# A two-layer network and a long convolution on one core: when the filter's first matrices are requested, in which order a block's rows are scaled, which engine writes zero rows, and where the plan pauses

## The chip, the core and the metric

The kernel runs on one core of one Trainium2 chip. The core has TensorE (matrix multiplication, with a weight load ahead of each product), VectorE, ScalarE, GpSimd, and SyncE, which here only issues DMAs. The profile calls them PE (weight loads PEld), DVE, ACT, POOL and SP. Each engine takes its instructions in an order that is fixed when the program is built, and waits for semaphores of the others.

The metric is the device time of one execution in microseconds, lower is better.

## The reference

With x of 2048 rows and 576 columns, all in float32:

```python
x = A_q
xn = _layernorm(x, axis=-1)
return x + _A_ref(xn, A_k, A_v, A_shift_k, A_ssm_k, A_ssm_D) + _B_ref(xn, B_w1, B_w2)
```

`_B_ref` is `relu(xn @ w1) @ w2` with w1 of 576 x 4608 and w2 of 4608 x 576. `_A_ref` is a gated long convolution: k goes through a causal convolution of four taps per column, the result is multiplied by v, then convolved per column over all 2048 rows with the filter `ssm_k` (the reference does so by an FFT of 4096 points), `ssm_D` times its input is added, and q, here the normalized x, multiplies the result.

## The kernel before, in words

**Number format.** Each float32 operand of TensorE is split into a high and a low part, and a product is made of three matmuls (high x high, high x low, low x high). ScalarE writes the high part, VectorE or, for weights, GpSimd the low part (`split_lo`, line 417).

**The layers.** Rows stand in four blocks of four tiles of 128 rows (`BT`). A visit (the loop of line 1130) takes one block through 256 of the 4608 columns of w1: `mm1` (line 538) for blocks 0 and 1, or `quad` (line 566), which saves products by sums of quarters, for blocks 2 and 3. `relu` (line 526) splits the result. `unit` (line 593) then multiplies 128 rows with a half of w2 (288 columns) and adds the sum onto `acc`; `done["acc"]` is the latest of these sums, `done["act"]` the latest ScalarE step of a visit.

**The first two blocks.** `first_xT` (line 231) centres and turns block 0 at the start. `second_xT` (line 279) does so for block 1 during the second visit: four rows are scaled by `normalized` (line 186) over all 576 columns, one after the other; then `turned` (line 267) transposes one column block of 128 of all four rows on TensorE into a bank, and `split_low` (line 210) writes its high part on ScalarE (line 219) and its low part on VectorE (line 220). Later blocks go through `later_xT` (line 292), in steps spread over many visits.

**The convolution** is a generator, `conv` (line 670), with four stages that run between the matmuls of the layers:
- the filter's transform (lines 709 to 766): `ssm_k` is loaded in twelve pieces, three matrices are requested by `load_const` (line 645) from GpSimd's queue, and after a pause 64 steps of `first` (line 656) follow, each of two matmuls, with a further matrix requested after each pair;
- the rows' transform (lines 769 to 847): `tap` makes the short convolution on VectorE (lines 788, 791, 792), `gate` multiplies by v (line 797), `split` writes the operands (lines 807 to 814), and `first` transforms them. The first loads for it (`first_loads`, line 702, and `load`, line 691) are emitted shortly before the end of the stage ahead. For the three rows before the start, `load` writes a zero into the first partition (line 698) and loads the rest;
- the middle (lines 850 to 951): 34 passes with products (line 879) over the transforms of filter and rows;
- the way back (lines 954 to 1033): `load_z` and `load_rest` fetch operands, lines 1020 and 1021 multiply them, `gate` and `add` finish.

**The plan.** `tick` (line 1045) is called after each six or seven matmuls of the layers with their columns as cost. It advances the clock and, where the convolution has credit, takes at most one step of the generator. A step that yields a positive number spends that many units of credit; one that yields a negative number stops the generator until so many columns of layer work have gone by. A unit of credit accrues at `rate` (line 1038):

```python
rate = FFT_TOTAL / (SHARE * FFN_TOTAL - PAUSES * PAUSE - START)
```

So the W_ constants (line 55) set how the convolution's steps are spread, and the pauses where it holds still. `PAUSE` is 16000 columns.

**Order.** The program's order of emission is a priority: the builder lets each engine take the earliest emitted instruction that it holds ready, and this fixes the engine's order. `tc.issue_after(x)` puts the instructions in its block behind x on x's engine; `here()` (line 664) puts them behind the latest sum on VectorE and the latest ScalarE step. A one-column memset in front of a DMA, as on line 715, ties that DMA to such a place, since the DMA then has to wait for it.

Of the kernel before, what the change touches and what calls it, by code (L numbers as in the profile page):

```python
# [17 lines left out]
P = 128  # L18
S = 2048
D = 576  # L20
# [3 lines left out]
NH = D // 2  # L24
# [7 lines left out]
BT = T // NB  # L32
# [5 lines left out]
U = S // (T * A1)  # L38
# [10 lines left out]
PAUSE = 16000  # L49
# [2 lines left out]


N_FK, N_FX, N_FM, N_FO = 4 * T, 4 * T, 6 * NG, 4 * T
W_FK, W_FX, W_FM, W_FO = 1.25, 4.7, 1.55, 2.35
Q = 32
KB = 3
KT_GAP = 2000
PAUSES = 4 * NH // Q // KB * KT_GAP / PAUSE + 13
FFT_TOTAL = N_FK * W_FK + N_FX * W_FX + N_FM * W_FM + N_FO * W_FO  # L60
W_QUAD = sum(W_STAGE)
FFN_TOTAL = NPAIR * HB * (W_PLAIN + W_QUAD + 2 * 4 * W_UNIT)
# [47 lines left out]
def h3_ffn_kernel(ctx: ExitStack, tc, x, k, v, shift_k, ssm_k, ssm_D, w1, w2, fwd, inv, mid, out):  # L110
    nc = tc.nc
# [16 lines left out]
    mv = const.tile([P, T, 2], F32, name="mv")  # L128
    rstd = const.tile([P, T], F32, name="rstd")
# [39 lines left out]
    def stats(t, src):  # L169
        st = xp.tile([P, 2, 6], F32, tag="bn", name=f"bn{t}", bufs=4)  # L170
        for h in range(2):
            nc.vector.bn_stats(st[:, h, :], src[:, h * NH:(h + 1) * NH])
        nc.vector.bn_aggr(mv[:, t, :], st)

    def inv_std(t0, n):

        q = xp.tile([P, 3, BT], F32, tag="q", name=f"q{t0}")[:, :, :n]
        va, h0, qu = q[:, 0, :], q[:, 1, :], q[:, 2, :]
        nc.vector.tensor_scalar(va, mv[:, t0:t0 + n, 1], EPS, None, op0=OP.add)
        nc.scalar.activation(h0, va, AF.Sqrt, scale=0.25)  # L180
        nc.vector.reciprocal(qu, h0)
        nc.vector.tensor_tensor(qu, va, qu, OP.mult)
        nc.vector.scalar_tensor_tensor(qu, qu, 0.25, h0, op0=OP.mult, op1=OP.add)
        nc.vector.reciprocal(rstd[:, t0:t0 + n], qu)

    def normalized(dst, src, t):
        nc.vector.tensor_scalar(dst, src, mv[:, t, 0:1], rstd[:, t:t + 1],
                                op0=OP.subtract, op1=OP.mult)

    def centred(dst, src, t):  # L190
# [7 lines left out]
    def f32(t):  # L198
        return t.bitcast(F32)
# [23 lines left out]
    def row_tiles(s, name):  # L223
        t = scratch(s, name)
        return [t[:, i * D:(i + 1) * D] for i in range(BT)]

    def plain_tiles(s):
        for name in ("b1", "b2", "xr"):
            operand(s, name)
# [37 lines left out]
    def turned(c, xn):  # L267
        w = min(P, D - c * P)
        ps = fft_psum()
        for i in range(BT):  # L270
            nc.tensor.transpose(ps[:w, i * P:(i + 1) * P], xn[i][:, c * P:c * P + w], ident)
        return ps
# [6 lines left out]
    def second_xT(srcs):  # L279

        plain_tiles(1)
        with tc.issue_after(done["acc"].ins):
            for t in range(BT + 2, HT):
                stats(t, srcs[t])
            inv_std(BT, BT)
        xn = row_tiles(1, "xn1")
        for i, row in enumerate(xn):
            normalized(row, srcs[BT + i], BT + i)
        for c in range(5):
            split_low(c, turned(c, xn), 1)  # L290

# [350 lines left out]
            unit(*args)  # L642
            room -= size

    def load_const(pool, src, name):
        w = pool.tile([P, 2, P], F32R, tag="wt", name=name, bufs=3)
        nc.gpsimd.dma_start(w, src)
        return w

# [13 lines left out]
    @contextmanager  # L663
    def here():


        with tc.issue_after(done["acc"].ins), tc.issue_after(done["act"].ins):
            yield

    def conv():  # L670
# [5 lines left out]
        with hold_pool as kp:  # L676
# [3 lines left out]
            win, gates, sums, uses = {}, {}, {}, [0]  # L680

            def slot(i):
                return both[:, i * D:(i + 1) * D]
# [7 lines left out]
            def load(t):  # L691
                win[t] = slot(WIN + t % (KS + 1))
                if t >= 0:
                    move(win[t], k, t, queues=(nc.sync, nc.sync))
                    gates[t] = slot(GATE + t % 2)
                    move(gates[t], v, t, queues=(nc.sync, nc.sync))
                else:
                    nc.vector.memset(win[t][0:1, :], 0.0)
                    nc.sync.dma_start(win[t][1:A1, :], k[1, 0:A1 - 1, T + t, :])
                    nc.sync.dma_start(win[t][A1:, :], k[0, :, T + t, :])  # L700

# [7 lines left out]
            with tc.tile_pool(name="fk", bufs=2) as fp:  # L709
                skip = fp.tile([P, NH], F32, tag="z", name="skip", bufs=3)  # L710
                for h in range(2):
                    nc.sync.dma_start(skip[h * A1:h * A1 + 1, :], ssm_D[None, h * NH:(h + 1) * NH])
                for b in range(0, NH // Q, KB):
                    with here():
                        nc.vector.memset(kr[:, b:b + KB, :1], 0.0)  # L715
                    for q in range(4):
                        h, r = divmod(q, 2)
                        src = ssm_k[h * NH + b * Q:h * NH + (b + KB) * Q, r * 32 * A2:(r + 1) * 32 * A2]
                        nc.sync.dma_start(kr[q * Q:(q + 1) * Q, b:b + KB, :],
                                          src.rearrange("(b d) l -> d b l", d=Q))  # L720
                        yield -KT_GAP
                ws = {}
                for n in range(3):
                    ws[n] = load_const(fp, fwd[n // U][:, n % U], f"wk{n}")
                yield -PAUSE
                turned_ = {}

                def transpose(i):
                    t2 = order[i]
                    pool, tag = (xp, "m5") if i % 2 else (fp, "tr")  # L730
                    tr = turned_[i] = pool.tile([P, NH], F32, tag=tag, name=f"tr{t2}", bufs=1)
                    with here():
                        nc.vector.transpose(tr.rearrange("p (b q) -> p b q", q=Q),
                                            kr.rearrange("p b (q t) -> p b q t", t=A2)[:, :, :, t2])
                        if t2 == 0:
                            for h in range(2):
                                row = slice(h * A1, h * A1 + 1)
                                nc.vector.tensor_tensor(tr[row, :], tr[row, :], skip[row, :], OP.add)

                def prepare(i, h):  # L740
                    if h == 0:
                        transpose(i)
                    stk = fp.tile([P, NH], F32R, tag="stk", name=f"ks{order[i]}_{h}", bufs=3)
                    with here():
                        stack(stk, turned_[i], h)
                    return stk

                order = [T * u + t for t in range(T) for u in range(U)]
                nxt = []
                for h in range(2):  # L750
                    nxt.append(prepare(0, h))
                    yield -PAUSE / 8
                for n, t2 in enumerate(order):
                    stk, nxt = nxt, []
                    u, t = divmod(t2, T)
                    for h in range(2):
                        z = fp.tile([P, NH], F32, tag="z", name=f"zk{t2}_{h}", bufs=3)
                        first(ws[n], stk[h], z, u)
                        nc.sync.dma_start(zk[:, t2, h * NH:(h + 1) * NH], z)
                        if n + 1 < len(order):  # L760
                            nxt.append(prepare(n + 1, h))
                        yield W_FK
                    if n + 2 == len(order):
                        first_loads()
                    if n + 3 < len(order):
                        ws[n + 3] = load_const(fp, fwd[(n + 3) // U][:, (n + 3) % U], f"wk{n + 3}")


            with tc.tile_pool(name="fx", bufs=2) as fp:
# [43 lines left out]
                            own, other = halves(u)  # L813
                            nc.sync.dma_start(f32(stks[t, u])[other], sums[t][own])

                yield -4 * PAUSE
                for n in range(KS):
                    tap(0, n)
                    yield -PAUSE / 4
# [7 lines left out]
                for t in range(T):  # L827
# [7 lines left out]
                    for u in range(U):  # L835
                        for h in range(2):
                            cols = slice(h * NH, (h + 1) * NH)
# [7 lines left out]
                        n = U * t + u + 3  # L845
# [4 lines left out]
        with tc.tile_pool(name="fm", bufs=2) as fp:  # L850
# [44 lines left out]
            for g in range(NG + 2):  # L895
# [10 lines left out]
                for h in range(2):  # L906
                    if g < NG:
                        ps, cols = run(*parts["k", g], 0, h)
# [6 lines left out]
                if 0 <= xg < NG:  # L915
                    k1, k2 = ks_.pop(xg)
                    sw = fp.tile([P, D], F32, tag="sw", name=f"sw{xg}", bufs=1)
                    for h in range(2):
                        ps, cols = run(*parts["x", xg], 0, h)
# [10 lines left out]
                for h in range(2):  # L930
                    if back is not None:
                        ps, cols = run(*back, 1, h)
# [21 lines left out]
        with tc.tile_pool(name="fo", bufs=2) as fp:  # L954
# [48 lines left out]
                load_z(n)  # L1003
            for i in range(2):
                load_rest(i)
            yield -3 * PAUSE / 2
            for n, (t, u) in enumerate(units):
                i = n // U
                w = rest[i][0]
# [5 lines left out]
                for h in range(2):  # L1015
# [3 lines left out]
                    cols = slice(h * NH, (h + 1) * NH)  # L1019
# [14 lines left out]


    stream = conv()
    clock = {"ffn": 0.0, "conv": 0.0, "until": START, "done": False}
    rate = FFT_TOTAL / (SHARE * FFN_TOTAL - PAUSES * PAUSE - START)

# [90 lines left out]
    for q, (n, s) in enumerate(visits):  # L1130
# [3 lines left out]
        if q == 1:  # L1134
            fill()
            second_xT(acc)
# [65 lines left out]
```

## Time and profile before

| | us |
|---|---|
| median of 3 runs | 1076.67 |
| lowest and highest | 1075.96, 1077.86 |
| the profiled execution | 1073.58 |
| its span, first to last instruction | 1071.8 |
| VectorE, ScalarE, GpSimd busy in the span | 753.2, 548.4, 394.1 |

The span leaves out what lies before the first and after the last instruction of the program, so it is shorter than the time of the same execution. The profile is of one execution, and the median is of others, so a term found in the profile is a difference that is applied to the median. In the page's rows a line such as L610 is line 610 of the kernel, `a<-b` names the tile written and the tile read, and a bracket in a timeline gives the idle time of the engine ahead of that instruction and what ended it. Matmuls overlap in the profile: one of 288 columns shows some 0.29 us, while a run of 24 takes 3.19 us.

### The profile page before, as it was taken

How to read it: one execution, taken by the hardware profiler on the slowest of the kernel's cores; microseconds unless marked ns; L12 is line 12 of the kernel's file. 1: busy time of each engine (PE TensorE's matmuls, PEld its weight loads, DVE VectorE, ACT ScalarE, POOL GpSimd, SP SyncE). 2: the span in 40 equal slices, each digit the busy share in tenths (PEclk: the TensorE clock that was granted, in tenths of full speed). 3: DMA queues.
4: the chain of work that ended last, by engine and by line, in shares of the span. 5: the costliest groups of instructions: out<-in, count | busy, mean ns of one | idle time of the engine just before them, and what ended most of it. 6: DMA issues, size and time to landing. Idle time of an engine off the chain costs nothing.

```text
span 1071.8 us, 19954 instructions
## 1 busy us (share of the span) xinstructions
PE 1051.1 (98%) x7147; PEld 988.1 (92%) x7147; DVE 753.2 (70%) x1310; ACT 548.4 (51%) x1201; POOL 394.1 (37%) x395
## 2 busy tenths in 40 slices
PE   8999999999999999999999999999999999999998
PEld 5799999889899999999999999999999999999997
DVE  5437878889777787762487777787878774566764
ACT  4224566535333344332386777777787763443430
POOL 4122333233222223233434434443434343544541
PEclk9999999999999999999999999999999999999999
DMA  8564867787847656855985556655655647977834
GB/s 215 125 160 127 223 159 197 199 260 205 211 139 207 185 170 193 247 154 184 315 233 180 159 156 180 191 170 168 191 162 162 182 122 242 315 246 221 239 124 111
DMA packets 156303, 204.45 MB, mean 191 GB/s; under 512 B 32845, under 2 KB 122703, under 8 KB 155180
## 3 DMA queue, kind: packets, MB, share of 16 engines
q1 hardware_dynamic: 143308, 189.00, 59.6%
q0 software_dynamic: 12576, 13.44, 5.4%
q8 instruction: 56, 0.92, 0.4%
q10 hardware_dynamic: 320, 0.74, 0.3%
q14 instruction: 43, 0.35, 0.1%
HBM read 133.92 MB, written 55.05 MB: 176 GB/s over the span
## 4 chain that ended last, share of the span: by engine, by line
PE 86%; DMA 7%; DVE 2%; ACT 1%; issue 1%; SPq 1%; POOL 0%; POOLq 0%; DVEq 0%; ACTq 0%
PE pso L610 38%; PE psh L547 20%; PE psb L523 12%; PE psf L879 6%; PE psa L523 5%; PE psf L660 3%; DMA zo<-zy 1%; DMA r<-in_w 1%; DMA both<-in_k 1%; DMA b<-kept_b 1%; DMA xt<-in_x 1%; PE psf L1020 1%; DMA ztk<-zk 1%; PE psf L1021 1%; DMA fin<-acc 1%
## 5 line engine op out<-in xcount | busy, mean ns | idle before, releaser
L610 PE MATMUL pso<-w,hh 128*128 128x288 f32 x2304 | 469.1, 295 | 2.1 <-DVE acc L614 1.6
L610 PEld LDWEIGHTS pso<-w,hh 128*128 128x128 f32 x2304 | 372.8, 188 | 11.4 <-DVE acc L614 2.3
L610 PE MATMUL pso<-w,ll 128*128 128x288 f32 x1152 | 328.1, 295 | 0.5 <-DVE both L715 0.5
L418 POOL TENSOR_TENSOR g<-r,g 128x256 fp32r<-128x256 f32 (+2 forms) x145 | 168.8, 1169 | 402.1 <-ACT g L447 326.5
L547 PE MATMUL psh<-b,g 128*128 128x512 f32 x864 | 217.8, 395 | 0.9 <-ACT b L219 0.7
L610 PEld LDWEIGHTS pso<-w,ll 128*128 128x128 f32 x1152 | 212.7, 188 | 1.5 <-DVE both L715 0.7
L547 PEld LDWEIGHTS psh<-b,g 128*128 128x128 f32 x864 | 157.1, 188 | 31.5 <-ACT b L219 1.2
L618 DVE TENSOR_TENSOR acc<-pso,acc 128x288 f32<-128x288 f32 x224 | 98.6, 450 | 69.3 <-PE pso L610 68.1
L418 POOL TENSOR_TENSOR w<-r,w 128x576 fp32r<-128x576 f32 x72 | 113.6, 1578 | 54.6 <-ACT w L509 54.4
L529 ACT ACTIVATE hh<-psh 128x512 fp32r<-128x512 f32 x72 | 43.0, 598 | 145.2 <-PE psh L547 145.0
L530 DVE SCALAR_TENSOR_TENSOR ll<-psh,hh 128x512 fp32r<-128x512 f32 x72 | 49.5, 688 | 69.3 <-ACT hh L529 69.1
L523 PE MATMUL psb<-t,g 128*128 128x256 f32 x648 | 95.0, 281 | 0.3 <-DVE psa L578 0.3
L447 ACT ACTIVATE g<-r 128x256 fp32r<-128x256 f32 (+2 forms) x145 | 76.7, 542 | 26.2 <-DMA r<-in_w 18.5
L523 PEld LDWEIGHTS psb<-t,g 128*128 128x128 f32 x648 | 85.4, 188 | 0.8 <-DVE psa L578 0.7
L476 POOL TENSOR_TENSOR r<-r 128x256 f32<-128x256 f32 x72 | 59.4, 845 | 44.5 <-DMA r<-in_w 43.3
L523 PE MATMUL psa<-b,g 128*128 128x256 f32 x432 | 63.4, 281 | 0.3 <-ACT psa L574 0.3
L523 PE MATMUL psb<-b,g 128*128 128x256 f32 x432 | 58.6, 281 | 0.0
L523 PEld LDWEIGHTS psa<-b,g 128*128 128x128 f32 x432 | 56.8, 188 | 0.6 <-ACT psa L574 0.6
L523 PEld LDWEIGHTS psb<-b,g 128*128 128x128 f32 x432 | 54.9, 188 | 0.0
L922 DVE TENSOR_TENSOR k<-psf,k 128x288 f32<-128x288 f32 x64 | 29.0, 454 | 33.8 <-ACT sw L921 32.1
L614 DVE SCALAR_TENSOR_TENSOR acc<-pso,rstd,acc 128x288 f32<-128x288 f32 x80 | 40.6, 511 | 16.8 <-PE pso L610 16.3
L529 ACT ACTIVATE hh<-psa 128x512 fp32r<-128x512 f32 x36 | 21.5, 596 | 53.8 <-PE psa L523 53.5
(133 smaller groups left out, 1684.2 us busy)
## 6 DMA issues: line engine op xcount, KB each, us to landing
r<-in_w SPq DMA_DIRECT2D x72, 288.0 KB, 3.6
zy<-vo SPq DMA_DIRECT2D x64, 288.0 KB, 3.2
zo<-zy SPq DMA_DIRECT2D x32, 576.0 KB, 5.6
r<-in_w SPq DMA_DIRECT2D x35, 512.0 KB, 4.0
zk<-zk SPq DMA_DIRECT2D x64, 144.0 KB, 2.6
ztk<-zk SPq DMA_DIRECT2D x32, 288.0 KB, 3.0
ztx<-zx SPq DMA_DIRECT2D x32, 288.0 KB, 3.2
k<-k SPq DMA_DIRECT2D x64, 144.0 KB, 3.0
```

The costliest lines, as they stand in the source:

```text
L418: return nc.gpsimd.tensor_tensor(dst, src, hi, OP.subtract)
L447: nc.scalar.activation(hi, src, AF.Copy)
L476: nc.gpsimd.tensor_tensor(dst, a, b, op)
L523: nc.tensor.matmul(ps, a, m, start=start and i == 0, stop=i == len(seq) - 1, skip_group_check=not start)
L529: done["act"] = nc.scalar.activation(hh, ps, AF.Relu)
L530: lows.append(nc.vector.scalar_tensor_tensor(ll, ps, 0.0, hh, op0=OP.max, op1=OP.subtract))
L547: nc.tensor.matmul(ps, a, m, start=i == 0, stop=i == len(seq) - 1)
L610: nc.tensor.matmul(ps[:, :NH], a, m, start=c == 0, stop=c == len(seq) - 1)
L614: done["acc"] = nc.vector.scalar_tensor_tensor(acc[t][:, dc], ps[:, :NH], rstd[:, t:t + 1], acc[t][:, dc], op0=OP.mult, op1=OP.add)
L618: done["acc"] = nc.vector.tensor_tensor(acc[t][:, dc], ps[:, :NH], acc[t][:, dc], OP.add)
L660: nc.tensor.matmul(ps[:, :NH], w[:, n, :], stk, start=n == 0, stop=n == 1)
L879: nc.tensor.matmul(ps[:, :NH], a, m[:, cols], start=n == 0, stop=n == 2)
```

## The change

Five things are altered. `load_const` gets a switch `late`, with which a one-column memset on VectorE, placed behind the latest sum, comes ahead of the request; the filter's first three matrices use it. `second_xT` scales the leading 128 columns of all four rows first, and then the other 448 of each. The memset of the zero rows goes from VectorE to GpSimd. Two pauses are longer by half a `PAUSE` each, ahead of the short convolution and ahead of the way back, and `PAUSES`, the constant that the rate takes off for them, is larger by one. The weights of a step of the filter's transform and of the rows' transform go from 1.25 to 1.3 and from 4.7 to 4.65.

```diff
-W_FK, W_FX, W_FM, W_FO = 1.25, 4.7, 1.55, 2.35
+W_FK, W_FX, W_FM, W_FO = 1.3, 4.65, 1.55, 2.35
...
-PAUSES = 4 * NH // Q // KB * KT_GAP / PAUSE + 13
+PAUSES = 4 * NH // Q // KB * KT_GAP / PAUSE + 14
...
-    def normalized(dst, src, t):
-        nc.vector.tensor_scalar(dst, src, mv[:, t, 0:1], rstd[:, t:t + 1],
+    def normalized(dst, src, t, cols=slice(0, D)):
+        nc.vector.tensor_scalar(dst[:, cols], src[:, cols], mv[:, t, 0:1], rstd[:, t:t + 1],
                                 op0=OP.subtract, op1=OP.mult)
...
         xn = row_tiles(1, "xn1")
-        for i, row in enumerate(xn):
-            normalized(row, srcs[BT + i], BT + i)
+        for cols in (slice(0, P), slice(P, D)):
+            for i, row in enumerate(xn):
+                normalized(row, srcs[BT + i], BT + i, cols)
...
-    def load_const(pool, src, name):
+    def load_const(pool, src, name, late=False):
         w = pool.tile([P, 2, P], F32R, tag="wt", name=name, bufs=3)
+        if late:
+            with here():
+                nc.vector.memset(f32(w)[:, 0, :1], 0.0)
         nc.gpsimd.dma_start(w, src)
         return w
...
-                    nc.vector.memset(win[t][0:1, :], 0.0)
+                    nc.gpsimd.memset(win[t][0:1, :], 0.0)
...
-                    ws[n] = load_const(fp, fwd[n // U][:, n % U], f"wk{n}")
+                    ws[n] = load_const(fp, fwd[n // U][:, n % U], f"wk{n}", late=True)
...
-                yield -4 * PAUSE
+                yield -9 * PAUSE / 2
...
-            yield -3 * PAUSE / 2
+            yield -2 * PAUSE
```

## The prediction

> **What bounds the kernel now.** First the head of the page: engines, clock, and the chain that ended last.
>
> ```profile
> span 1071.8 us, 19954 instructions
> PE 1051.1 (98%) x7147; PEld 988.1 (92%) x7147; DVE 753.2 (70%) x1310; ACT 548.4 (51%) x1201; POOL 394.1 (37%) x395
> PEclk9999999999999999999999999999999999999999
> PE 86%; DMA 7%; DVE 2%; ACT 1%; issue 1%; SPq 1%; POOL 0%; POOLq 0%; DVEq 0%; ACTq 0%
> ```
>
> TensorE is busy in 1051.1 of 1071.8 us at its full granted clock, and 86% of the chain is matmuls. The change removes no matmul, so all it can win lies in the 20.7 us in which TensorE stood, and some of those are the fill at the front and the last stores. Where they stand is read from the windows (columns: the stretch, its length, then TensorE, its weight loads, VectorE, ScalarE and GpSimd busy, clock, DMA share and GB/s) and from TensorE's own list of waits (total, times, longest).
>
> ```profile
> 0.00:13.50 13.50, 9.69 (x47) 5.06 (x47) 3.41 (x10) 6.04 (x12) 5.97 (x14) 1.00 0.93 225
> 13.50:34.00 20.50, 16.75 (x89) 13.18 (x90) 17.70 (x50) 6.67 (x15) 5.87 (x5) 1.00 0.86 209
> 205.00:275.00 70.00, 67.03 (x399) 60.21 (x398) 61.64 (x97) 29.41 (x60) 22.71 (x22) 1.00 0.83 243
> 520.00:890.00 370.00, 367.76 (x2797) 361.62 (x2796) 280.53 (x484) 263.41 (x589) 151.11 (x129) 1.00 0.59 176
> 890.00:1055.00 165.00, 162.51 (x1240) 159.50 (x1239) 101.98 (x190) 65.13 (x150) 80.10 (x91) 1.00 0.74 227
> ```
>
> ```profile
> PE psf L1020 <- DMA zo<-zy: 2.0, 2, 1.3
> PE psf L271 <- DVE xn L187: 1.5, 1, 1.5
> PE psf L660 <- DMA xs<-both: 1.5, 1, 1.5
> PE psf L879 <- DVE k L922: 1.1, 1, 1.1
> ```
>
> TensorE stood 3.75 us in 13.5 to 34 (the first blocks), 2.97 in 205 to 275 (the turn from the filter's transform to that of the rows), 2.24 in 520 to 890 and 2.49 in 890 to 1055 (the transform back). Three of the four largest waits quoted lie where an edit of this change lies. So this is a change of a few us, worked out wait by wait.
>
> **Next block's rows in two column groups (lines 186 and 287).** Columns of a timeline: start, length, engine, line, and in brackets the idle time before.
>
> ```profile
> 28.62 0.16 DVE L179 TENSOR_SCALAR q<-mv 128x4 f32<-128x4 f32 x1
> 30.63 2.05 DVE L187 TENSOR_SCALAR xn<-acc,mv,rstd 128x576 f32<-128x576 f32 x4
> 31.27 2.02 PE L271 MATMUL psf<-ident,xn 128*128 128x128 f32 x12 [1.52 <-DVE xn L187]
> 33.10 1.58 ACT L219 ACTIVATE b<-psf 128x512 fp32r<-128x512 f32 x3 [4.08 <-PE psf L271]
> 33.73 1.89 DVE L220 TENSOR_TENSOR b<-psf,b 128x512 fp32r<-128x512 f32 x3 [1.05 <-ACT b L219]
> 33.76 0.74 PE L547 MATMUL psh<-b,g 128*128 128x512 f32 x2 [0.47 <-ACT b L219]
> ```
>
> Four scalings at 2.05/4 = 0.51 us a row go one by one; the first 128 columns are turned as each row comes, so column block 0 is whole only after row 4, at 32.68, and ScalarE starts at 33.10. Afterwards there are eight scalings. The fixed part is near the 0.16 us of the 4-column row; 128 columns are then about 0.16 + 0.35 x 128/576 = 0.24 at most, pitch about 0.2, so four end near 31.5 and ScalarE can start near 31.7. The other four have 448 columns at about 0.43: VectorE ends near 33.15 rather than 32.68, so 0.4 us is added. What is late next is VectorE: the low half of block 0 (line 220) stands behind these four in its queue, so it starts near 33.15 rather than 33.73. TensorE has at most the hi products before that. Gain: 33.73 - 33.15 = **0.6 us**. The bounds: a loss of 0.4 if the order of the rest stays as it is, a gain of 1.5 if all of the quoted wait goes. Column blocks 1 to 4 come 0.4 us later, behind matmuls that already run.
>
> **The filter's first matrices (lines 645 and 724).** What moves are three GpSimd DMA issues of 128 KB; three small memsets are added.
>
> ```profile
> 3.62 1.63 POOL L647 DMA_DIRECT2D wk<-in_fwd  x3
> 10.26 0.82 DVE L172 BATCH_NORM_STATS2 bn<-acc 128x6 f32<-128x288 f32 x2 [2.28 <-DMA acc<-in_x]
> q10 hardware_dynamic: 155, 0.59, 27.9%
> q0 software_dynamic: 103, 0.29, 15.4%
> L660 PE MATMUL psf<-ks,wk x128: 291/295/401, 84.0 to 210.6; 128*128 128x288 f32 x128
> DMA to landing us min/median/max: 2.3/3.1/7.9
> ```
>
> The two queue rows are those of the DMA view for 0 to 9 us (packets, MB). GpSimd's queue had moved 0.29 MB by then, less than the 0.33 MB of weight pieces (256 KB and twice 32 KB, lines 429 and 431) issued ahead of these matrices, so none of them was in flight; ScalarE's queue had moved its 0.59 MB, both its x loads whole. So the x that VectorE waited 2.28 us for did not share its data time with them. They delay what comes behind: the second weight piece, second layer weights, rows of block 1. VectorE is busy 17.70 of 20.50 us in 13.5 to 34 on what has landed, so earlier landings shorten nothing there: **0** (a gain of 1.75 us at most: 0.39 MB at 225 GB/s, the mean of the first 13.5 us). Issued near 67 us (the planner's place, layer matmul 240 by count in the timeline), they have 17 us to the first use at 84.0, against 7.9 us for the slowest landing. GpSimd's 1.63 us is behind the 13.5 to 34 rush. Cover gone, the filter's first step would slip by what is missing, with first-layer matmuls to take its place.
>
> The Trainium skill, "DMA: Bandwidth & Descriptors", section "Queues, rings and completion order", has each DMA engine take its queues in turn, packet by packet. By that rule the three requests do take time from SyncE's queue beside them, and the start would be up to 1.75 us shorter if that queue carried what is awaited; the two queue rows speak against it for the x loads.
>
> **Zero rows by GpSimd (line 698).**
>
> ```profile
> 0.74 0.20 POOL masks.py:197 MEMSET ident<- 128x128 f32 x1 [0.29 <-POOLq L1182]
> 205.02 1.75 DVE L698 MEMSET both<- 1x576 f32 x3
> 207.99 0.76 DVE L788 TENSOR_TENSOR both<-both 128x576 f32<-128x576 f32 x1 [1.22 <-DMA both<-in_k]
> 209.38 0.94 DVE L654 TENSOR_TENSOR ks<-tr,ks 64x288 fp32r<-64x288 f32 x2
> 209.88 0.53 PE L660 MATMUL psf<-ks,wk 128*128 128x288 f32 x2 [0.65 <-DVE ks L654]
> ```
>
> 1.75 us leave VectorE, then it waits 1.22 us for the k rows in any case. TensorE's 0.65 us goes if the last filter rows (line 654) take the freed place ahead of that first product. The product also goes behind sums emitted 26 matmuls later (next part), which favours this. I take **0.5**. The bounds: a loss of 2.0 us, and a gain of 0.65. On GpSimd the three cost 0.20 x 576/128 = 0.9 us each at most; what is queued behind are weight splits due a visit later.
>
> The loss comes from the nearest row of GpSimd in VectorE's way:
>
> ```profile
> 198.28 2.43 DVE L394 TENSOR_TENSOR area<-area 128x256 f32<-128x256 f32 x1
> 198.97 1.45 POOL L418 TENSOR_TENSOR w<-r,w 128x576 fp32r<-128x576 f32 x1
> 240.76 0.41 DVE L394 TENSOR_TENSOR area<-area 128x256 f32<-128x256 f32 x1
> ```
>
> The same subtraction takes 2.43 us beside a GpSimd subtraction and 0.41 alone: 2.0 us. The Trainium skill, "SBUF — State Buffer", section "SBUF: two separate sides", says that a VectorE operation with two SBUF inputs blocks only against a GpSimd operation that reads SBUF. By that rule a memset, which reads none, costs VectorE's products nothing, and the lower bound would be 0; no row here shows a GpSimd memset beside a VectorE product.
>
> **The planner's weights and pauses (lines 55, 59, 816, 1006).** The rate is FFT_TOTAL over (SHARE x FFN_TOTAL - PAUSES x PAUSE - START). FFT_TOTAL stays 828.8 (64 x 0.05 is added and taken away), the denominator falls by one PAUSE from 1,669,057 columns, so the rate rises by 0.97%. I stepped the clock through its ticks for both versions, which is counting, and number the 6120 layer matmuls in order. The filter's transform stays where it is (at most one step goes in a tick); the first product of the rows goes from matmul 918 to 944, the first row transform from 1134 to 1158, the fourth row pair from 1286 to 1317; from the tenth they are level. The middle ends at 4820 rather than 4850; the first step back stays at 4944. The end is 6 matmuls earlier, the last third unforced.
>
> ```profile
> 217.99 0.76 DVE L791 TENSOR_TENSOR both<-both 128x576 f32<-128x576 f32 x1 [1.09 <-DMA both<-in_k]
> 220.50 0.53 PE L610 MATMUL pso<-w,hh 128*128 128x288 f32 x2 [0.84 <-DVE acc L614]
> 271.04 0.50 PE L660 MATMUL psf<-xs,wx 128*128 128x288 f32 x2 [1.48 <-DMA xs<-both]
> 64.79 3.19 PE pso L610 x24
> ```
>
> A matmul of 288 columns is 3.19/24 = 0.133 us, so 26 are 3.5 us. *Longer pause ahead of the rows.* At 217.99 VectorE waits for k with a sum behind it, for which TensorE then stands 0.84. 3.5 us of delay would cover that wait, but these products run late already (matmul 918, the plan's place for the first, starts some ten us before 207.99 by count) and go as data come: I take half, **0.4** (0 to 0.84). At 271.04 the fourth pair's operand lands 1.48 us late, after a burst that keeps VectorE busy 61.64 of 70 us. Its step moves by 31 matmuls, those before by 24 to 26: some 5 x 0.133 = 0.7 us of slack more, and the later burst meets less of the work on the later blocks' rows (line 292). I take **0.9** (0 to 1.48).
>
> *Longer pause ahead of the way back.*
>
> ```profile
> 901.64 8.10 DMA zo<-zy
> 900.04 0.40 PE L1020 MATMUL psf<-zo,wi 128*128 128x288 f32 x1 [0.23 <-DMA wi<-in_inv]
> 909.88 0.37 PE L1020 MATMUL psf<-zo,wi 128*128 128x288 f32 x1 [1.30 <-DMA zo<-zy]
> ```
>
> The chain shows the load that TensorE waits for at 909.88 as 8.10 us long. Loads start when the middle's last result is stored, some 26 to 30 matmuls, 3.5 to 4.0 us, earlier, while the fourth unit's step keeps its place: the 1.30 goes, the first step's 0.23 and the later 0.7 of that kind may stay. I take **1.3** (0 to 2.2).
>
> *Price of the denser middle.* 34 passes lose 30 x 0.133 = 4.0 us of room, 0.12 each; VectorE is at 280.53 of 370 there. With every order after the edits drawn anew, I put **+0.9** for waits that come up elsewhere (0 to 5.5, below).
>
> **Sum.** -0.6 - 0 - 0.5 - 0.4 - 0.9 - 1.3 + 0.9 = -2.8 us. The profiled execution took 1073.58 us, 1.78 outside its span of 1071.8; it becomes 1070.8. The runs' median, 1076.67, stands 3.09 above that execution, so the forecast is 1076.67 - 2.8 = **1073.9 us**, 0.26% faster. About 0.2% (2.15 us) is what a measurement of this kernel can tell from no change.
>
> **Rivals.** *The waits form anew* at the next transfer: each DMA wait returns, a transfer earlier or later, and only 0.6 + 0.5 of the front and the zero rows stay, less the 0.9: 1076.5 us, the same. For it: loads there take 8 us wherever they start, and steps that lag the plan go when data come. Against it: later units of the same loops run without a wait. Chance 0.34, with the case that the split does not do what it says (VectorE takes the low half after all eight scalings as before).
>
> *The denser middle waits.* One wait for VectorE's product (line 922) is 1.1 us. If five more of the 34 passes catch it, 5.5 us come back: -3.7 + 5.5 = +1.8; from six, 6.6 - 3.7 = +2.9, 1079.6 us and slower. It decides from the sixth pass on. Against it: only this one is in the list now, and VectorE has 24% left there. Chance 0.10.
>
> *The first requests do slow the start:* 1.75 us more, 1072.2 us. For it: transfers fill the DMA engines then. Against it: the two queue rows. Chance 0.08, on the faster side.
>
> **How the numbers follow.** Forecast 0.48, waits anew 0.34, slow middle 0.10, faster start 0.08. Faster 0.56 in all; a little of the forecast's lower edge falls within 0.2%, so 0.54, the same 0.36, slower 0.10. All gains at their bounds (1.5, 0.65, 0.84, 1.48, 2.2) sum to 6.7, so 1070.0 is the low end; the high end takes in part of the slow middle, 1078.6.
>
> **What would show it.** Right: ScalarE's first split of block 1 (line 219) near 31.7 and VectorE's (line 220) near 33.1; no long wait near 905 to 910; the wait on xs below 0.6; the filter's first matrices issued near 67 with line 660 still from 84. Wrong: line 220 later than 33.7, waits of over 1 us on zo or xs again, line 879 standing over 3 us in all, or a TensorE front that starts line 547 before 13.0.

## The result and the profile after

| | runs | median us | lowest to highest |
|---|---|---|---|
| before, beside the changed kernel | 13 | 1077.86 | 1072.39 to 1081.08 |
| the changed kernel | 13 | 1070.88 | 1067.98 to 1075.77 |

The ratio is 0.995, with a 95% interval of 0.9932 to 0.9968: faster by 0.5%, about 5.4 us (3.4 to 7.3), where the forecast was 2.8. The two medians lie 6.98 us apart, inside that interval. The median of 1070.88 lies in the range that was put on record, but near its low end, 1070.0, which stood for all gains at their bounds. The profiled execution took 1072.73 us, 0.85 less than that of before, and its granted clock had a mean of 0.994 against 0.999. It is one of the slower executions of its kernel, which the readings below have to allow for.

First the head of the page after, with its chain that ended last, and the same windows as before (columns as there):

```profile
span 1071.0 us, 19976 instructions
PE 1054.1 (98%) x7147; PEld 991.6 (93%) x7147; DVE 748.2 (70%) x1314; ACT 549.7 (51%) x1201; POOL 397.5 (37%) x398
PE 92%; DMA 3%; DVE 3%; ACT 1%; issue 1%; SPq 0%; ACTq 0%; DVEq 0%
```

```profile
13.50:34.00 20.50, 17.42 (x85) 13.43 (x82) 16.90 (x51) 6.39 (x14) 5.86 (x5) 0.92 0.74 183
205.00:275.00 70.00, 69.23 (x416) 62.68 (x416) 61.63 (x96) 30.37 (x62) 23.43 (x24) 1.00 0.81 233
520.00:890.00 370.00, 369.05 (x2812) 363.20 (x2811) 280.14 (x486) 265.27 (x592) 154.25 (x133) 1.00 0.62 183
890.00:1055.00 165.00, 162.25 (x1229) 159.54 (x1229) 102.17 (x189) 64.04 (x148) 77.06 (x88) 0.99 0.69 212
```

TensorE stands 16.9 us of the span rather than 20.7, and matmuls make up 92% of the chain rather than 86%. In the turn (205 to 275) it stands 0.77 us rather than 2.97, in the middle (520 to 890) 0.95 rather than 2.24. In the way back (890 to 1055) it stands 2.75, no less than the 2.49 of before, though one of the two longer pauses was meant for it. TensorE's own list of waits after (total, times, longest) says what is left:

```profile
PE psf L255 <- DVE xn L193: 3.0, 1, 3.0
PE psf L1024 <- DMA zo<-zy: 2.7, 2, 2.3
PE psf L271 <- DVE xn L187: 1.3, 1, 1.3
PE psf L664 <- DVE ks L658: 0.8, 1, 0.8
```

The wait on `xs` and the one on the middle's `k` are out of the list; line 1024, 1020 before, still waits for `zo`. (Lines after are 1 to 4 higher than before: 610 is 611, 654 is 658, 660 is 664, 922 is 926, 1020 is 1024.)

Why 3.8 us less standing gave only 0.85 us in these two executions shows in TensorE's busy time, which is 3.0 us longer, and in the clock. The windows of three short stretches after follow; in the profile of before no stretch of this length has a lowered clock.

```profile
14.00:17.50 3.50, 3.30 (x7) 2.38 (x8) 3.09 (x5) 3.50 (x9) 1.81 (x3) 0.52 0.87 200
34.60:38.00 3.40, 3.40 (x14) 3.00 (x15) 1.99 (x5) 1.35 (x4) 0.00 (x0) 0.50 1.03 216
905.00:908.40 3.40, 3.40 (x17) 3.40 (x17) 0.32 (x1) 0.67 (x3) 0.06 (x1) 0.50 0.69 258
```

Three times TensorE runs for about 3.4 us at half its clock, each time within 2 us of a wait of the list (those of lines 255, 271 and 1024, which end at 12.63, 32.88 and 903.83), and "busy" counts that as work. If TensorE sets the pace there, half of 3.4 us is 1.7 us lost for each, an estimate. Four other executions of the same kernel had a mean clock of 1.0 and took 1068.2 to 1070.88 us. So a single profile is read here for where TensorE stands, and only the rounds of runs tell what an edit is worth.

### The profile page after: what moved, and what is told of

The parts are those of the page before. It is cut to its first block, busy times and chain, and to the rows that moved or that the text cites. A ratio compares the mean times of both kernels' runs of the same rounds, so it can differ in the third digit from the quotient of the medians.

```text
span 1071.0 us, 19976 instructions
## 1 busy us (share of the span) xinstructions
PE 1054.1 (98%) x7147; PEld 991.6 (93%) x7147; DVE 748.2 (70%) x1314; ACT 549.7 (51%) x1201; POOL 397.5 (37%) x398
## 4 chain that ended last, share of the span: by engine, by line
PE 92%; DMA 3%; DVE 3%; ACT 1%; issue 1%; SPq 0%; ACTq 0%; DVEq 0%
PE pso L611 41%; PE psh L548 22%; PE psb L524 12%; PE psf L883 7%; PE psa L524 6%; PE psf L664 3%; DMA zo<-zy 1%; DMA acc<-in_x 1%; PE psf L1024 1%; PE psf L1025 1%; DMA both<-in_k 0%; DVE bn L172 0%; PE psf L271 0%; ACT k L914 0%; ACT k L913 0%
```

## The experiments

The theory under test was that of the forecast: the two pauses give the time, because loads and VectorE's sums get a lead ahead of TensorE; the three local edits give little. The rivals: the local edits do it; the weights of line 55 do it; the order drawn anew does it, whichever edit causes it. All ratios are to the kernel before, run in the same rounds.

| run | edit, from | runs | ratio (95%) |
|---|---|---|---|
| e1_plan_undone | plan as before, local edits stay | 12 | 1.000 (0.9983 to 1.0016) |
| e2_plan_alone | before, plan of after | 12 | 0.9948 (0.993 to 0.9966) |
| e3_one_group | after, rows scaled whole | 10 | 0.9951 (0.9935 to 0.9967) |
| e4_early_requests | after, requests early | 7 | 0.9947 (0.9927 to 0.9967) |
| e6_first_pause_back | after, first pause as before | 12 | 0.9976 (0.9956 to 0.9996) |
| e7_back_pause_back | after, back pause as before | 12 | 0.9992 (0.9972 to 1.0012) |
| e8_old_weights | after, weights as before | 7 | 0.9935 (0.9911 to 0.9959) |
| e10_deeper_loads | after, one load more ahead on the way back | 6 | 0.9915 (0.9895 to 0.9936) |
| e11_first_pause_5 | after, first pause half a PAUSE longer still | 12 | 0.9959 (0.9945 to 0.9973) |
| e11b_back_pause_25 | after, back pause half a PAUSE longer still | 12 | 0.9961 (0.994 to 0.9981) |
| e12_deeper_short_pause | e10 with the back pause as before | 5 | 0.992 (0.9903 to 0.9937) |

Beside them, e9_before_again is one more profile of the kernel before. The changed kernel and e2, e3, e4 and e8 all have both longer pauses; weighted by their intervals they come to 0.9947, and about 0.0016 is taken to either side, the width of the narrowest of them, since several share their runs of before. The single undone edits are set against that.

### The plan undone, and the plan alone

The first takes the plan back in the changed kernel; the second puts only the plan into the kernel before.

```diff
 e1: the changed kernel with
-W_FK, W_FX, W_FM, W_FO = 1.3, 4.65, 1.55, 2.35
+W_FK, W_FX, W_FM, W_FO = 1.25, 4.7, 1.55, 2.35
-PAUSES = 4 * NH // Q // KB * KT_GAP / PAUSE + 14
+PAUSES = 4 * NH // Q // KB * KT_GAP / PAUSE + 13
-                yield -9 * PAUSE / 2
+                yield -4 * PAUSE
-            yield -2 * PAUSE
+            yield -3 * PAUSE / 2
 e2: the kernel before with the same four lines the other way
```

> The changed kernel with the old weights and pauses of the plan; row groups, late requests and GpSimd zero rows stay. Theory A (most of the gain is the plan: the waits near 220 and 271 us go because the first pause is longer): both waits come back, 1.0 to 1.7 us each, the time is 0.25% to 0.5% above the changed kernel's, some 0.1% below that of before. Theory B (the gain is local, from the start and the row groups): the time stays within 0.1% of the changed kernel's and TensorE stands less than 1 us in 215 to 300 us.

> The kernel before with the new weights and pauses alone. Theory A: 0.3% to 0.45% faster than before, no wait over 0.5 us in 215 to 300 us, the waits in the filter's middle (520 to 880 us) below 5 us as in the changed kernel. Theory B: within 0.1% of before, waits of over 1 us at 220 or 271 us remain.

e1 is level with before, and e2 with the changed kernel. So the plan carries the whole gain, and the three local edits together are worth 0 within 0.17% (1.8 us). TensorE's waits in e1:

```profile
PE psf L664 <- DMA xs<-both: 2.9, 2, 2.3
PE psf L1024 <- DMA zo<-zy: 1.6, 1, 1.6
PE pso L611 <- DVE acc L615: 1.4, 3, 0.6
```

With the short pauses the waits of before are back: on `xs` (2.31 us at 271), and on the sum of line 615 in the turn (0.60 at 220).

The profile of e2 does not show what was expected of it. Its execution took 1077.42 us, the slowest of e2's twelve, and with the longer pauses TensorE waits for `xs` at 253 and at 266 us (1.83 and 2.44):

```profile
PE psf L1024 <- DMA zo<-zy: 5.5, 2, 3.5
PE psf L664 <- DMA xs<-both: 4.3, 2, 2.4
```

So that the plan brings the gain rests on the times of e1 and e2, not on waits that always go.

### Rows in one group, and early requests

```diff
 e3
-        for cols in (slice(0, P), slice(P, D)):
+        for cols in (slice(0, D),):
 e4
-                    ws[n] = load_const(fp, fwd[n // U][:, n % U], f"wk{n}", late=True)
+                    ws[n] = load_const(fp, fwd[n // U][:, n % U], f"wk{n}")
```

> The changed kernel with the four rows scaled over all 576 columns in one go. Theory A: the 0.74 us wait of line 548 behind the transposes comes back, 0.5 us (0.05%) slower than the changed kernel. Rival (the second group's delay eats the gain): within 0.2 us of it in TensorE's waits of 30 to 36 us.

> The changed kernel with the filter's first matrices requested at the start again. Theory A: the first real matmuls start as before, the x loads of rows 2 and 3 land between 10.1 and 10.9 us either way, time within 0.1%. Rival (the requests slow the start): TensorE's first product of block 0 starts 0.5 to 1.75 us later than in runs with late requests, 0.05% to 0.16% slower.

Both come out at the changed kernel's ratio, to 0.0003, with intervals of 0.0016 and 0.002 to either side, so terms of 0.5 or of 1.75 us can't be told from 0 by the time. What the groups do at their place is in the timelines (start, length, line) of the changed kernel, then of e3:

```profile
32.48 2.81 DVE L187 TENSOR_SCALAR xn<-acc,mv,rstd 128x128 f32<-128x128 f32 x8
34.02 0.60 ACT L219 ACTIVATE b<-psf 128x512 fp32r<-128x512 f32 x1 [3.15 <-PE psf L271]
34.79 1.20 PE L548 MATMUL psh<-b,g 128*128 128x512 f32 x2
35.20 0.68 DVE L220 TENSOR_TENSOR b<-psf,b 128x512 fp32r<-128x512 f32 x1
```

```profile
30.96 2.05 DVE L187 TENSOR_SCALAR xn<-acc,mv,rstd 128x576 f32<-128x576 f32 x4
33.42 1.58 ACT L219 ACTIVATE b<-psf 128x512 fp32r<-128x512 f32 x3 [4.08 <-PE psf L271]
34.05 1.89 DVE L220 TENSOR_TENSOR b<-psf,b 128x512 fp32r<-128x512 f32 x3 [1.05 <-ACT b L219]
34.07 0.74 PE L548 MATMUL psh<-b,g 128*128 128x512 f32 x2 [0.47 <-ACT b L219]
```

Counted from the start of the scaling, ScalarE's split begins after 1.54 us in two groups and 2.46 in one, VectorE's after 2.72 and 3.09. The groups do what they say, and bring VectorE's split 0.37 us nearer. TensorE's waits on lines 271 and 548 come to 1.5 and 0.9 us in e3, and to 1.3 and 0.2 in the changed kernel.

For the early requests the starts tell more than the time. TensorE's first product of block 0 starts at 13.65 us in e4 and at 14.20 in the changed kernel. Over all fourteen profiles it starts between 13.01 and 13.65 with early requests (before, e2, e4, e9) and between 13.16 and 14.20 with late ones. So late requests do not bring the start forward.

### Each pause by itself

```diff
 e6
-PAUSES = 4 * NH // Q // KB * KT_GAP / PAUSE + 14
+PAUSES = 4 * NH // Q // KB * KT_GAP / PAUSE + 13.5
-                yield -9 * PAUSE / 2
+                yield -4 * PAUSE
 e7
-PAUSES = 4 * NH // Q // KB * KT_GAP / PAUSE + 14
+PAUSES = 4 * NH // Q // KB * KT_GAP / PAUSE + 13.5
-            yield -2 * PAUSE
+            yield -3 * PAUSE / 2
```

> The changed kernel with the pause ahead of the short convolution back at 4 PAUSE (PAUSES 13.5, so that the rate fits). Theory T1 (the gain is made at the turn, where the row products come 26 layer matmuls later): nearly all of the gain goes, ratio to before 0.998 to 1.0, waits on xs or on sums of over 1 us in 215 to 300 us. Theory T2 (the gain is the lead of the loads ahead of the way back) or T3 (the faster pace through the middle): ratio stays 0.994 to 0.996.

> The changed kernel with the pause ahead of the way back at 1.5 PAUSE again (PAUSES 13.5). T1: ratio to before stays 0.994 to 0.996, no wait over 0.5 us in 215 to 300 us. T2: 0.998 to 1.0, waits on zo of over 3 us in all after 890 us. T3: between, the middle being 14 matmuls ahead of before and not 26.

e7 came out as the theory of the back pause had it, and its `zo` waits at 4.1 us in all; e6 fell between what its two theories gave. Against 0.9947, undoing the first pause costs 0.0029 and undoing the second 0.0045, each to about 0.0026: 3.1 and 4.8 us. That is more together than the whole 0.5%, so each is partly worth something only with the other, or the true sizes lie at the low ends of these intervals. The first has its place in the trace, in the window of the turn and the timeline of e6:

```profile
205.00:275.00 70.00, 65.58 (x395) 59.16 (x394) 58.58 (x93) 29.57 (x61) 21.09 (x22) 1.00 0.83 236
```

```profile
222.13 0.53 PE L611 MATMUL pso<-w,hh 128*128 128x288 f32 x2 [1.64 <-DVE acc L615]
273.68 0.51 PE L664 MATMUL psf<-xs,wx 128*128 128x288 f32 x2 [2.21 <-ACT g L448]
```

TensorE stands 4.42 us in the turn. It waits 1.64 for the sum at 222, where before waited 0.84, and 2.21 at 274, the place of the old wait on `xs` (named here after a ScalarE step). Standing time in the turn, worked out from this window in each kernel's profile: with the short first pause 2.97 (before), 2.71 (e9), 3.55 (e1), 4.42 (e6); with the long one 0.77 (after), 1.04 (e3), 1.17 (e4), 0.77 (e7), 1.12 (e8), 1.13 (e10), 1.95 (e11b), but 2.59 in e12 and 4.54 in e2, where waits on `xs` have come up at earlier pairs. So there is less standing in most executions with the long pause, not in all.

The second pause has no such plain place. In the way back TensorE stands 2.49 (before), 3.04 (e9), 2.04 (e1) and 4.40 (e7) with the short pause, and 2.75 (after), 5.50 (e2), 2.46 (e3), 3.43 (e4), 3.80 (e6), 3.56 (e8), 4.01 (e11), 5.81 (e11b) with the long one: no less. Which loads TensorE waits for says why. The fourth unit's load is the one of before's 1.30 us; after, the loads of the fourth and the fifth unit are requested at these times, and the wait is for the fifth:

```profile
887.39 0.60 SPq L970 DMA_DIRECT2D zo<-zy  x1
896.34 0.33 SPq L970 DMA_DIRECT2D zo<-zy  x1
903.83 0.37 PE L1024 MATMUL psf<-zo,wi 128*128 128x288 f32 x1 [2.31 <-DMA zo<-zy]
```

The fourth unit's request, at 901.64 before, has come 14 us forward, and its products do not wait. Counted the same way (two products of line 1024 a unit), the first wait on `zo` is for the fourth unit in the three profiles with both pauses short (before, e1, e9: 1.30 to 1.65 us), for the fifth with one pause longer or both (after, e2, e3, e4, e6, e7, e8, e11: 0.97 to 2.44) and for the sixth with a back pause of 2.5 (e11b: 1.97). Ten of these twelve profiles have a second one at the thirtieth unit, 0.38 to 3.46 us. So longer pauses do not take the wait away; they move it to a later unit.

What e7's profile shows is one long wait and what follows on it, in the timeline and the windows:

```profile
1015.67 0.37 PE L1024 MATMUL psf<-zo,wi 128*128 128x288 f32 x1 [3.17 <-DMA zo<-zy]
```

```profile
1012.00:1016.00 4.00, 0.83 (x6) 0.63 (x6) 0.69 (x1) 1.30 (x3) 2.69 (x4) 1.00 1.04 319
1016.00:1019.40 3.40, 3.40 (x16) 3.21 (x15) 0.37 (x1) 1.00 (x2) 0.12 (x1) 0.50 0.55 220
```

3.17 us of waiting, then 3.4 us at half clock: 4.9 us from one late load. But one execution doesn't tell how often that happens, and e2 has such a wait (3.46 us at 1024) with the long pause.

### The weights

```diff
-W_FK, W_FX, W_FM, W_FO = 1.3, 4.65, 1.55, 2.35
+W_FK, W_FX, W_FM, W_FO = 1.25, 4.7, 1.55, 2.35
```

> The changed kernel with step weights 1.25 and 4.7 of before, longer pauses kept. By the planner's count only the third and fourth row pairs move, by 7 and 12 matmuls earlier. T1 to T3 alike: ratio to before stays 0.994 to 0.996. Rival (the weights space the burst of the row transforms): a wait on xs of over 1 us near 270 us and a ratio of 0.997 or more.

0.9935 against 0.995, with intervals of about 0.002 to either side: the new weights bring no gain that shows, and the rival that they did it falls. So does that of the order drawn anew: e2, e3, e4 and e8 are four programs with both longer pauses, each with an order of its own, and all lie between 0.9935 and 0.9951.

### Before, once more

> The kernel before once more, unaltered, for a second profile of it. If the waits of the first profile are the program's, then the wait on k with a sum behind it near 220 us, the wait on xs near 271 us and the waits on zo near 910 and 1020 us are there again, each within 0.5 us; if they are chance of one execution, some are gone or over 1 us longer, and single profiles can't carry terms of 1 us.

```profile
PE pso L610 <- DVE acc L614: 2.7, 3, 1.9
PE psf L1020 <- DMA zo<-zy: 2.6, 2, 1.4
PE psf L660 <- DMA xs<-both: 1.6, 2, 0.8
```

The waits on which the forecast rested stand in the same instructions, so they belong to the program. Their sizes don't: the sum at 221 cost 1.9 us here and 0.84 before, the operand at 271 0.8 rather than 1.48. Of the four only the first `zo` wait (1.38 rather than 1.30) came within the 0.5 us expected. A wait read from one execution is good to no better than about 1 us.

### One load more ahead on the way back

If the back pause earns by giving the `zo` loads a lead, a fifth buffer and one more load in flight should give the same, and with it the pause should be worth less. (`low` gives up a buffer to make room; that was not run by itself.)

```diff
 e10
-                    z = fp.tile([P, 2, D], F32R, tag="zt", name=f"zo{n}", bufs=4)
+                    z = fp.tile([P, 2, D], F32R, tag="zt", name=f"zo{n}", bufs=5)
-            for n in range(3):
+            for n in range(4):
                 load_z(n)
-                low = fp.tile([P, D], F32, tag="low", name=f"low{t}_{u}")
+                low = fp.tile([P, D], F32, tag="low", name=f"low{t}_{u}", bufs=1)
-                        load_z(n + 3)
+                        load_z(n + 4)
 e12: e10 with
-PAUSES = 4 * NH // Q // KB * KT_GAP / PAUSE + 14
+PAUSES = 4 * NH // Q // KB * KT_GAP / PAUSE + 13.5
-            yield -2 * PAUSE
+            yield -3 * PAUSE / 2
```

> The changed kernel with the loads on the way back one unit further ahead: five buffers for zo and not four, requests at n + 4, and one buffer for low to make room. Theory L (TensorE waits on the way back because zo is requested too late, 8 us ahead of its landing): the waits on zo fall from 2.3 to 3.6 us in all to below 1, the half clock behind them goes, and the time is 1.5 to 4 us below the changed kernel's: ratio to before 0.991 to 0.994. Rival (the transfers are limited by what else moves, so an earlier request lands no earlier): waits on zo stay above 2 us, ratio 0.994 to 0.996, or above where the one buffer for low costs.

> The kernel with the deeper loads on the way back, and the pause ahead of the way back at 1.5 PAUSE again (PAUSES 13.5). With four buffers, putting this pause back cost 0.42% of the time. Theory L (the longer pause earns by giving the loads their lead, which the fifth buffer gives as well): putting it back costs less than 0.2% now, ratio to before 0.991 to 0.9935, waits on zo below 2 us. Rival (the pause earns in another way, by where the middle and the way back fall): it costs 0.35% or more again, ratio 0.995 to 0.998.

e10 is the best version of the study: 0.9915, its highest run (1069.58 us) below the changed kernel's median in other rounds. Its window of the way back and its waits:

```profile
890.00:1055.00 165.00, 163.87 (x1254) 161.56 (x1253) 106.09 (x193) 64.94 (x147) 77.24 (x86) 1.00 0.69 212
```

```profile
PE psf L1024 <- DMA zo<-zy: 1.1, 1, 1.1
```

TensorE stands 1.13 us there, and 1.31 in e12; none of the kernels with four buffers stands less than 2.04. One wait of 1.1 us is left, now for the sixth unit (in e12 too, 1.05 us), where the changed kernel had two of 2.7 in all and e2 two of 5.5; neither e10 nor e12 has one at the thirtieth. The loads themselves are no faster. The last row of the view of the tile `zo`, after and then e10:

```profile
DMA to landing us min/median/max: 3.7/5.1/8.5
```

```profile
DMA to landing us min/median/max: 3.7/5.9/10.2
```

They land later after issue, and are waited for less: here the lead counts, not the transfer time. Against 0.9947 the fifth buffer brings 0.0032, to about 0.0026.

With the fifth buffer, taking the pause back costs 0.0005 (interval about 0.0027 to either side), without it 0.0045 (about 0.0026). The two intervals overlap; their difference, 0.0040 to about 0.0037, is only just clear of 0. That would fit a pause that earns by giving the loads a lead, but no profile shows it: the first wait on `zo` is 0.97 us with the short back pause (e7) and 1.04 to 2.44 for the same unit with the long one. What the back pause gives stays open.

### Longer pauses still

```diff
 e11 and e11b, each with
-PAUSES = 4 * NH // Q // KB * KT_GAP / PAUSE + 14
+PAUSES = 4 * NH // Q // KB * KT_GAP / PAUSE + 14.5
 e11
-                yield -9 * PAUSE / 2
+                yield -5 * PAUSE
 e11b
-            yield -2 * PAUSE
+            yield -5 * PAUSE / 2
```

> The changed kernel with the first pause at 5 PAUSE (PAUSES 14.5): the first product of the rows moves from matmul 944 to 962, the first row transform from 1158 to 1172. Theory T1 with a threshold (the wait goes once the products come after the landing of k, which they do at 4.5 but for the first): the wait of line 664 on ks near 212 us (1.0 us) goes, ratio to before 0.993 to 0.995. Rival (order only): the wait at 212 stays, ratio 0.994 to 0.997.

> The changed kernel with the pause ahead of the way back at 2.5 PAUSE (PAUSES 14.5): the middle ends 30 matmuls earlier again, the first step back keeps its place. Theory T2 (lead of the loads): the gain from 1.5 to 2 (0.26% to 0.42% of the time by the two runs with one pause put back) goes on, ratio to before 0.990 to 0.994. T2 with saturation: 0.994 to 0.996, waits on zo as before. Rival T4 (the denser middle takes it back): 0.996 or more, waits of line 883 above 3 us.

Neither gains on the changed kernel, and both lie outside what their own theories gave for a further gain. In e11b the waits on `zo` are three, 5.3 us in all, and line 883, which the rival named, is not in the list. TensorE's waits in e11:

```profile
PE psf L1024 <- DMA zo<-zy: 3.5, 2, 2.4
PE psf L664 <- DMA xs<-both: 2.7, 2, 1.6
```

The turn is again at 1.62 us of standing: the wait for `ks` at 212 is gone and one of 1.6 us on `xs` has come up at 254. Here too a half `PAUSE` more moves the wait along.

## Why the prediction came out as it did

The direction, and the pauses as the main source, were right; the sum was half of what came. The step that was mis-sized is the plan: -0.4 - 0.9 - 1.3 + 0.9 = -1.7 us, where e2, the plan alone, measured 0.52%, 5.6 us (3.7 to 7.5). The other terms, -1.1 together, measured 0 (e1), to 1.8 us, so the time does not refute them. That the median still fell into the range is in part luck: the low end adds up waits at their bounds, and that of the way back was not taken away.

**Rows in two groups: -0.6 predicted.** Right in mechanism: VectorE's eight scalings took 2.81 us (2.5 worked out), and VectorE's split follows after 2.72 us where 3.10 was the row of before: 0.4 us at the place. In the time it can't be told from 0 (e3). Line 220 started at 35.20, later than the 33.7 that was to show the term wrong, but the scaling itself began at 32.48 rather than 30.63.

**Late requests: 0 predicted.** Held as far as the runs can tell: e4 is level. The requests went out at 74.4 us, not near 67, and the first product that uses them started at 86.7. The view of their line after (shortest, median and longest ns; first and last start):

```profile
L651 POOL DMA_DIRECT2D wk<-in_fwd x32: 528/546/566, 74.4 to 199.9; - x32
```

The rival of the slow start has no support: the first product of block 0 started no earlier with the late requests. A gain of 1.75 us, 0.16%, lies within the intervals of the time.

**Zero rows: -0.5 predicted, wrong.** The step that failed is that the last filter rows take the freed place. The timeline of the turn after:

```profile
205.24 1.61 POOL L702 MEMSET both<- 1x576 f32 x3 [2.06 <-DVE tr L737]
210.17 0.76 DVE L792 TENSOR_TENSOR both<-both 128x576 f32<-128x576 f32 x1 [2.33 <-DMA both<-in_k]
211.56 0.94 DVE L658 TENSOR_TENSOR ks<-tr,ks 64x288 fp32r<-64x288 f32 x2
212.07 0.53 PE L664 MATMUL psf<-ks,wk 128*128 128x288 f32 x2 [0.77 <-DVE ks L658]
```

VectorE's product on the `k` rows still stands ahead of line 658 (654 before), and what the memset left became a longer wait for `k`: 2.33 rather than 1.22. TensorE's wait is 0.77 rather than 0.65. The edit wasn't undone by itself; e1, which keeps it, shows no gain, to 1.8 us. On GpSimd the three took 1.61 us, 0.54 each, under the bound of 0.9. The loss of up to 2.0 did not come there: VectorE's subtraction of line 658 that began at 205.21, beside the first memset, took 0.46 us, and the two at 211.56 took 0.94.

**First pause: -1.3 predicted; 3.1 by e6, 0.9 by e7 against e1 (with the weights), each to about 2.8.** The time doesn't refute the term. The profile after speaks for a discount that was too large (half of the 0.84, 0.9 of the 1.48), since it has neither wait and TensorE stands 2.2 us less in the turn; those of e2 and e12, with waits on `xs` at other pairs, speak against a gain of the whole. With e9 and e6 the two waits of before come to 2.7 to 3.9 us rather than the 2.3 of its one profile.

**Back pause: -1.3 predicted; 4.8 by e7, 2.6 by e6 against e1 (with the weights).** The step as put, "the 1.30 goes", failed in the profile after. The lead came: the fourth unit's load was requested 14 us earlier and was not waited for. But the wait went on to the fifth unit, at 903.83 with 2.31 us, and in the way back TensorE stands 2.46 to 5.81 us with the long pause and four buffers, 2.04 to 4.40 with the short one. The size was wrong on the other side: by e7 the time gained 2 us or more, where 1.3 was the term; by e6 against e1 alone that is not shown. What pays for it stays open. The fifth buffer of e10 shows only that with one more load in flight most of the waits on `zo` go, and that the time is some 0.3% shorter.

**Denser middle: +0.9 predicted.** Not seen: TensorE stands 0.95 us there rather than 2.24, and the wait on line 922's product is gone. Among the other kernels the middle lies between 0.26 (e1) and 2.17 (e7) with either plan, so this isn't put down to an edit; a 0.9 to 1.25 us wait near 538 us is there with the rows in one group (before, e2, e3, e9), but in e10 too, and its cause stays open.

**The rivals.** Waits formed anew did occur, and as that rival put it, a transfer later: on `zo` from the fourth unit to the fifth, on `xs` in e2, e11 and e12. Yet the time fell, where it had 1076.5 us. The middle's rival, over 3 us on the product, did not occur. Left open: where the second pause's gain arises, and how it divides between waiting and clock. The mean clock over all runs was 0.9963 in e7, 0.9978 in the changed kernel and 0.9975 in before, so of e7's 4.8 us some 1.6 could be clock, while between before and after there is none to speak of.

## What to carry to other kernels

Where loads feed the bound engine, count how many of them are in flight against the slowest landing, and give the pool a buffer more before moving the schedule: here TensorE stood 1.13 and 1.31 us in the way back with a fifth buffer and 2.04 or more without, and the longer pause only moved the wait to a later unit. In a plan that spreads work, half a pause more ahead of a stage is worth trying at each turn; a further half showed no gain here, with waits at the next operands. Size such edits by rounds of runs, since one profile shows where the waits are, but each of them only to 1 us or worse: the largest of the list, on line 255, lies between 1.0 and 3.0 us over the fourteen profiles.

## What the hardware did that was not expected

A wait of 1.3 to 3.2 us can be followed by some 3.4 us in which TensorE has half its clock: after the waits of 3.0, 1.3 and 2.3 us of the changed kernel, and after the 3.17 us of e7. The windows of the changed kernel around its wait of 2.31 us are the two stretches 900 to 905, here, and 905 to 908.4, above:

```profile
900.00:905.00 5.00, 2.69 (x20) 2.28 (x19) 2.35 (x5) 2.16 (x5) 3.25 (x5) 1.00 1.07 383
```

e4 had the same wait of up to 2.3 us in an execution with a mean clock of 1.0, so it does not follow every time. The Trainium skill, "TensorE: Matmul & The Clock Gate", section "What's actually happening", has the clock either full or halved, decided over a free-running window of 3413 ns. The length of the stretches, and that the same wait triggers one in one execution and none in another, agree with that; that the clock is halved after an idle window of some 3.4 us does not, if idle means without work, as 2.31 us sufficed here with TensorE busy 2.69 of 5 us. It is also one reason why runs of one kernel lie up to 8 us apart: the changed kernel's four with a mean clock of 1.0 took 1068.2 to 1070.88 us, its five of 0.997 and less took 1071.74 to 1075.77; the four of 0.998 took 1067.98 to 1071.57, so it is not the only one.
